# A gated linear-attention layer and its feed-forward layer: joined first products for the first two pairs of stages, the v*s term in whole blocks, and stage 0's scores ahead of the next turning

## The chip, the cores and the metric

The kernel runs on one core of one Trainium2 chip. A core has five engines that run side by side and meet through semaphores: TensorE (PE: matmuls, with weight loads listed apart as PEld), VectorE (DVE), ScalarE (ACT), GpSimd (POOL) and SyncE (SP, which here only issues transfers). The metric is the device time of one execution in microseconds, lower is better. Of several executions the median counts.

## The reference

Four sequences with eight heads of 48 channels and 768 time steps go through a recurrent attention with per-channel decay `w` and a bonus `u` for the current step; the result, brought to 3072 tokens of 384 channels, goes through two matrix products with a leaky rectifier between them.

```python
def _attn_ref(r, k, v, w, u):
    B, H, S, D = r.shape            # 4, 8, 768, 48
    state = np.zeros((B, H, D, D), dtype=np.float32)
    y = np.zeros_like(r)
    for t in range(S):
        kt, vt, rt = (k[:, :, t].copy(), v[:, :, t].copy(), r[:, :, t].copy())
        cur = np.einsum('bhd,bhe->bhde', u[None] * kt, vt)
        y[:, :, t] = np.einsum('bhd,bhde->bhe', rt, state + cur)
        state = w[None, :, :, None] * state + np.einsum('bhd,bhe->bhde', kt, vt)
    return y.astype(np.float32)

def _moe_ref(x, w_in, w_out):       # x 3072x384, w_in 384x2048, w_out 2048x384
    h = x @ w_in
    g = np.maximum(0.01 * h, h)
    return (g @ w_out).astype(np.float32)
```

## The kernel before, in words

The 3072 tokens are cut into 24 stages of 128 tokens (`NST`), six to a sequence. Two stages make a pair, and the feed-forward layer works on pairs or single stages. Within a sequence the stages hang together by a 48x48 state for each head.

A stage n goes through these steps. Their letters stand in the order that is written out by hand in `ORDER`, which covers stages 0 to 9 (the first pairs); the later pairs run in a loop of the same steps.

- `P` (`prep`, DVE): r and k times tables of powers of w. Result `qk`.
- `T` (`turn`, PE and ACT): for stages 0 to 7, eight matmuls of 128x128 against the identity (line 379) turn `qk`, four for the k half and four for the q half; two copies bring the halves from PSUM to `tp`. All copies are ACT's (line 390), except the k half of stage 0, which is DVE's (line 387). From stage 8 on a DMA transpose does the turning.
- `A` (`a_mm`, PE): the scores, eight matmuls with 48 rows each (line 403), two at a time in the upper and lower half of the array.
- `X` (`diag`, DVE): the elementwise product q*k of the turned halves; `K` (`kv_mm`, PE) sums it over channels with the bonus (four matmuls of two columns, line 433), adds k^T v (four of 96 columns, line 437) and the carried state (line 442).
- `M` (`a_mask`, DVE): the scores from PSUM times a triangular mask (line 421), two instructions of 128x512.
- `Q` (`prep2`, DVE): `vs`, that is v times the per-token, per-head sum s from `K`. `S` (`state`, DVE): the next state.
- `Y` (`y_part`, with `y_mm`, PE and ACT): the attention output of the stage, already transposed, in one PSUM bank. Its matmuls have 32 output rows each, so the array is used as four columns of 32, and four of them run side by side: 16 with the scores, 12 with the state (none where a sequence begins), and for stages 0 to 7 another 12 that add `vs` against the identity. ACT then copies the bank to `xT` (line 537).
- `G n.g` (`g1`): a quarter of the first feed-forward product for one stage, 12 matmuls of 128 columns into one bank, and one ACT instruction (the rectifier, line 555). `J m.j` (`g1_pair`): an eighth of it for both stages of pair m, six matmuls of 256 columns (line 567) and one ACT instruction (line 573). Both fill a bank of 128x512, so a `J` replaces a `G` in bank, ACT work and multiplications. `G n.g` covers what `J m.2g` and `J m.2g+1` cover, for one of the two stages. `J` needs both halves of `xT`, and needs a quarter of `w_in` as `G` does.
- `H` (`g2`): the second product of a stage, 16 matmuls of 384 columns (line 584). From pair 5 on a form with seven half-size products (line 648) does it.
- `L` loads r, k and v of a later stage; the loads of the first eight stages and of the weights are issued by POOL in the order `LOADS`, before anything else. `C`, `W` and `U` make small tables.

Each engine runs its instructions in the order in which they are recorded, so a step that waits holds up all that stands behind it on its engine. A PSUM bank is taken in turn out of eight and must have been read before it is written again. Each matmul instruction carries a weight load of its own.

Of the kernel before, what the change touches and what calls it, by code (L numbers as in the profile page):

```python
# [6 lines left out]
AF = mybir.ActivationFunctionType  # L7
# [14 lines left out]
NSL = HD // 128  # L22
# [1 line left out]
FIRST, EARLY = 6, 2  # L24
LOADS = """r1 k1 r2 id k2 wi0 v1 r3 tri k3 v2 wi1 k4 r4 v3 wi2 k5 r5 r6 k6 v4 v5 k7 wi3 r7 v6 v7 wo3 wo2 wo1 wo0"""
ORDER = """
P0 C W T0 P1 T1 A0 X0 M0 P2 A1 K0 T2 Q0 X1 Y0 A2 S0 M1 K1 X2 G0.0 Q1 P3 S1 Y1 T3 K2 M2 G1.0 X3 A3 U G0.1 S2 G1.1 Q2 M3 Y2 K3 P4
T4 Q3 G2.0 G2.1 G0.2 S3 G2.2 G1.2 Y3 P5 A4 P6 X4 M4 T5 X5 G3.0 K4 Q4 A5 S4 T6 G3.1 K5 G3.2 Y4 M5 L8 Q5 Y5 P7 A6 G1.3 J2.0 J2.1 T7
M6 X6 X7 K6 J2.2 J2.3 A7 S6 J2.4 J2.5 L9 Q6 G2.3 G0.3 J2.6 M7 L10 J2.7 L11 G3.3 K7 S7 P8 Q7 Q8 P9 H0 Q9 K8 H1 P10 L12 K9 H2 S8 S9
Y6 Y7 A8 A9 P11 M8 H3 M9 L13  # L30
"""

# [5 lines left out]
class Sched:  # L38
# [7 lines left out]

    def add(self, eng, emit, R=(), W=(), dma=None):
        o = Op()
        o.eng, o.emit, o.dma, o.inc, o.val = eng, emit, dma, False, None
        deps = []  # L50
        for key in R:
            w = self.writer.get(key)
            if w is not None:
                deps.append((w, True))
        for key in W:
            w = self.writer.get(key)
            if w is not None:
                deps.append((w, False))
            for r in self.readers.get(key, ()):
                deps.append((r, False))  # L60
        o.deps = []
        for d, raw in deps:
            if d.dma is None and d.eng == eng and dma is None and (eng == "pe" or not raw):
                continue
            if d is not o and d not in o.deps:
                o.deps.append(d)
        for key in R:
            self.readers.setdefault(key, []).append(o)
        for key in W:
            self.writer[key] = o  # L70
            self.readers[key] = []
        self.ops.append(o)
        return o
# [47 lines left out]
def bass_rwkv5_eagle__then__act_leaky_relu_kernel(  # L121
# [13 lines left out]
    def SB(name, shape, dt=BF16):  # L135
        return ctx.enter_context(nc.sbuf_tensor(name, shape, dt))

    NQK, NTP, NVS, NAT, NT, NX, NG, NO, NRK = 6, 6, 6, 6, 6, 3, 3, 4, 14
    TURNED, DIAG = 8, 8
# [29 lines left out]
    ident = SB("ident", [128, 128])  # L169
# [4 lines left out]
    tp = [SB(f"tp{i}", [128, 2 * NP, 128]) for i in range(NTP)]  # L174
    vs = [SB(f"vs{i}", [128, HD]) for i in range(NVS)]
# [12 lines left out]
    V, A, PE, SP, G = nc.vector, nc.scalar, nc.tensor, nc.sync, nc.gpsimd  # L188
    sch = Sched(ctx, nc)
    add = sch.add  # L190
    taken = [0]

    def next_bank():
        i = taken[0] % 8
        taken[0] += 1
        return ps[i], ("ps", i)
# [12 lines left out]
    def load_one(n, which, pace=()):  # L209
# [7 lines left out]
        key = (which, n if which == "v" else n % NRK)  # L217
        add("pool", lambda: G.dma_start(dst, src), R=pace, W=[key], dma=f"{which}{n}")  # L218

# [30 lines left out]
    def fill(n):  # L250
# [6 lines left out]

        add("pe", emit, R=["ones"], W=[("ps", i), f"fill{n}"])

    half_w = [(next_bank(), slice(NH * i, NH * i + NH)) for i in range(2)]  # L260

    def identity():
        add("pool", lambda: G.affine_select(ident[:, :], ones[:, 0:128], pattern=[[1, 128]], compare_op=ALU.is_equal,
                                            fill=0.0, base=0, channel_multiplier=-1), R=["ones"], W=["ident"])

# [4 lines left out]
    for name in LOADS.split():  # L270
# [12 lines left out]
        R=["tcol"], W=["kexp"])  # L283
    add("dve", lambda: V.tensor_scalar(qexp[:, :], tcol[:, :], 1.0, float(-MID), ALU.mult, ALU.add),
        R=["tcol"], W=["qexp"])
    add("dve", lambda: V.memset(v_sb[:, :, :].rearrange("p n (h e) -> p (n h) e", e=E)[:, :, D:E], 0.0), W=["v0"])
    add("dve", lambda: V.tensor_tensor(wu_row[:, :], w_row[:, :], u_row[:, :], ALU.mult),
        R=["w_row", "u_row"], W=["wu_row"])
# [5 lines left out]
    for (ps_w, key_w), cols in half_w:  # L294
        add("pe", lambda ps_w=ps_w, cols=cols: PE.matmul(ps_w[:, 0:NH], one_row[:, :], w_row[:, cols], start=True, stop=True),  # L295
            R=["one_row", "w_row"], W=[key_w, "bc"])
    for i, ((ps_w, key_w), cols) in enumerate(half_w):
        add("act", lambda ps_w=ps_w, cols=cols: A.activation(lnw[:, cols], ps_w[:, 0:NH], AF.Ln), R=[key_w], W=[("lnw", i)])
        add("act", lambda cols=cols: A.activation(qtab[:, cols], lnw[:, cols], AF.Exp, scale=qexp[:, 0:1]),
            R=[("lnw", i), "qexp"], W=[("qtab", i)])  # L300
    add("act", lambda: A.activation(ktab[:, :], lnw[:, :], AF.Exp, scale=kexp[:, 0:1]),
        R=[("lnw", 0), ("lnw", 1), "kexp"], W=["ktab"])
# [68 lines left out]
    def turn(n):  # L371
        it, iq = n % NTP, n % NQK
        for half in ((0, 1) if n == 0 else (1, 0)):
            ps_t, key = next_bank()

            def emit(half=half, ps_t=ps_t):
                for p in range(NP):
                    h0 = half * H + 2 * p
                    last = PE.matmul(ps_t[:, 128 * p:128 * p + 128],  # L379
                                     qk[iq][:, h0:h0 + 2, :].rearrange("p h e -> p (h e)"), ident[:, :],  # L380
                                     start=True, stop=True)
                return last

            add("pe", emit, R=[("kp" if half else "qp", iq), ("qk0", iq), "ident"], W=[key])
            dst = tp[it][:, NP * half:NP * half + NP, :].rearrange("p m t -> p (m t)")
            if n == 0 and half == 1:
                add("dve", lambda dst=dst, ps_t=ps_t: V.tensor_copy(dst, ps_t[:, :]),  # L387
                    R=[key], W=[("tp", it, half)])
            else:
                add("act", lambda dst=dst, ps_t=ps_t: A.activation(dst, ps_t[:, :], AF.Copy),  # L390
                    R=[key], W=[("tp", it, half)])

    def a_mm(n):
        it = n % NTP
# [100 lines left out]
    def y_mm(n, ps_y, key):  # L495
        it, ia, iv, is_ = n % NTP, n % NAT, n % NVS, n % NT

        def column(q):
            todo = []
            for s in range(NSL):  # L500
                p, kk = divmod(4 * s + q, 3)
                c0 = 128 * p
                one = []
                if kk < 2:
                    one.append((v_sb[:, n, c0 + 32 * kk:c0 + 32 * kk + 32], at[ia][:, 0, p, :]))
                if kk > 0:
                    c1 = c0 + 16 + 32 * kk
                    one.append((v_sb[:, n, c1:c1 + 32], at[ia][:, 1, p, :]))
                if n % NC:
                    one.append((st[is_][:, p, 32 * kk:32 * kk + 32], tp[it][:, p, :]))  # L510
                if n < DIAG:
                    one.append((vs[iv][:, 128 * s + 32 * q:128 * s + 32 * q + 32], ident[:, :]))
                todo += [(s, a, m, i == 0, i == len(one) - 1) for i, (a, m) in enumerate(one)]
            return todo

        def emit():
            columns = [column(q) for q in range(4)]
            for step in range(max(len(x) for x in columns)):
                for q in range(4):
                    if step < len(columns[q]):  # L520
                        s, a, m, first_mm, last_mm = columns[q][step]
                        last = PE.matmul(ps_y[32 * q:32 * q + 32, 128 * s:128 * s + 128], a, m,  # L522
                                         start=first_mm, stop=last_mm)
            return last

        reads = [("v", n), "v0", ("at", ia, 0), ("at", ia, 1), "ident", ("tp", it, 0)]
        if n < DIAG:
            reads.append(("vs", iv))
        if n % NC:
            reads.append(("st", is_))  # L530
        add("pe", emit, R=reads, W=[key])

    def y_part(n):
# [203 lines left out]
    def u_table():  # L737
# [3 lines left out]
        add("act", lambda: A.activation(u_tab[:, :], ps_u[:, 0:HD], AF.Copy), R=[key], W=["u_tab"])  # L741

    steps = {"U": u_table, "P": prep, "Q": prep2, "T": turn, "A": a_mm, "M": a_mask, "K": kv_mm, "S": state, "Y": y_part, "X": diag, "C": decay_columns, "W": decay_table, "F": fill,
             "G": g1, "J": g1_pair, "H": g2, "L": lambda n: load_stage(n, pace=[("pace", (n - 4) // 2, (n - 4) % 2)])}
    for name in ORDER.split():
# [116 lines left out]
```

## Time and profile before

| what | value |
|---|---|
| median of the runs | 169.61 us (168.82 to 169.82, 3 runs) |
| profiled execution, its own time | 169.31 us |
| profiled execution, first to last instruction (span) | 167.6 us |
| PE | 159.8 us busy, 95% of the span, 2348 matmuls and 2348 weight loads |
| DVE, ACT, POOL | 120.7, 116.1 and 81.7 us busy |
| PE's share of the chain that ended last | 93% |
| data loaded and stored by DMA | 19.68 MB |

Busy time of PE is counted from the start of a matmul to its modelled end, and one matmul starts long before the one ahead of it ends. What PE really costs is therefore read from the distance between starts: in a row such as `18.12 0.83 PE L550 ... x12` the twelve starts are spread over 0.83 us less the length of the last one. Times within the execution are microseconds from the first instruction.

### The profile page before, as it was taken

To read this page: it belongs to the slowest core of one execution; us is meant where nothing else is said; L and a number is where in the kernel's file an instruction comes from. 1 tells how busy PE (TensorE), PEld (TensorE's weight loads), DVE (VectorE), ACT (ScalarE), POOL (GpSimd) and SP (SyncE) were. 2 spreads that over 40 slices of the span, in tenths; PEclk is the share of its full clock that TensorE was granted. 3 is DMA by queue.
4 is the path that set the end of the run, shared out by engine and by line. 5 is a ranking of instruction groups with operands and counts; after the bars stand their busy time and mean duration, and the time that the engine had idled before them with its cause. 6 is when DMAs were issued, how large, how long until landed. Compare 5 with 4: busy or idle time off the path is not lost.

```text
span 167.6 us, 5494 instructions
## 1 busy us (share of the span) xinstructions
PE 159.8 (95%) x2348; PEld 133.7 (80%) x2348; DVE 120.7 (72%) x232; ACT 116.1 (69%) x264; POOL 81.7 (49%) x97
## 2 busy tenths in 40 slices
PE   6679999979999999999999999999999999999994
PEld 3557898968766885886875889889899898898993
DVE  7768884853698969999449997986998477036253
ACT  4823888778323581689989889989999845828520
POOL 7999999990079979697570660840000000000000
DMA  5999999999999999989997996994507302002022
GB/s 100 112 149 172 171 152 173 202 187 143 116 123 208 109 139 75 151 150 102 203 157 42 219 124 49 215 120 77 147 0 98 125 4 94 4 0 94 4 94 94
DMA packets 99259, 19.68 MB, mean 117 GB/s; under 512 B 92322, under 2 KB 99236, under 8 KB 99236
## 3 DMA queue, kind: packets, MB, share of 16 engines
q0 software_dynamic: 76512, 10.03, 91.6%
q1 hardware_dynamic: 21682, 9.11, 26.4%
q8 instruction: 18, 0.29, 0.7%
q10 hardware_dynamic: 1042, 0.20, 0.6%
q14 instruction: 5, 0.04, 0.1%
HBM read 20.45 MB, written 4.72 MB: 150 GB/s over the span
## 4 chain that ended last, share of the span: by engine, by line
PE 93%; DVE 3%; issue 1%; ACT 1%; DVEq 0%; ACTq 0%
PE ps_all L567 31%; PE ps_all L648 20%; PE ps_all L584 16%; PE ps_all L522 7%; PE ps_all L550 7%; PE ps_all L403 4%; PE ps_all L379 3%; PE ps_all L437 3%; DVE qk L327 1%; DVE at L421 1%; PE ps_all L255 1%; PE ps_all L442 1%; PE ps_all L295 1%; PE ps_all L433 0%; DVE tp L387 0%
## 5 line engine op out<-in xcount | busy, mean ns | idle before, releaser
L567 PE MATMUL ps_all<-xT,w_in_sb 128*128 128x256 bf16 x480 | 54.5, 273 | 0.0
L567 PEld LDWEIGHTS ps_all<-xT,w_in_sb 128*128 128x128 bf16 x480 | 46.7, 98 | 5.8
L573 ACT ACTIVATE gT<-ps_all 128x512 bf16<-128x512 f32 x80 | 46.7, 595 | 5.7 <-PE ps_all L567 2.1
L218 POOL DMA_DIRECT2D rk_sb<-in_k_dram x23 | 21.7, 944 | 16.3 <-PE ps_all L567 16.3
L584 PE MATMUL ps_all<-w_out_sb,gT 128*128 128x384 bf16 x160 | 27.2, 326 | 0.0
L413 DVE CAST_PREDICATED at<-mask,ps_all 128x1024 bf16<-128x1024 uint16 x16 | 18.8, 1219 | 8.9 <-PE ps_all L403 8.9
L367 ACT ACTIVATE at<-ident,s_tok 128x128 bf16<-128x128 bf16 x80 | 24.8, 389 | 0.0
L584 PEld LDWEIGHTS ps_all<-w_out_sb,gT 128*128 128x128 bf16 x160 | 15.3, 98 | 9.7
L218 POOL DMA_DIRECT2D v_sb<-in_v_dram x24 | 22.7, 955 | 0.4 <-issue 0.4
L218 POOL DMA_DIRECT2D rk_sb<-in_r_dram x23 | 21.5, 939 | 0.0
L361 POOL TENSOR_TENSOR at<-ident,s_tok 128x512 bf16<-128x512 bf16 x12 | 13.4, 1142 | 11.6 <-DVE s_tok L351 11.6
L679 DVE TENSOR_TENSOR out_sb<-ps_all,snap 128x192 f32<-128x192 f32 x22 | 7.8, 356 | 14.5 <-PE ps_all L648 13.8
L648 PE MATMUL ps_all<-tw,gs 128*128 128x192 bf16 x168 | 16.0, 246 | 0.0
L590 ACT ACTIVATE out_sb<-ps_all 128x384 f32<-128x384 f32 x10 | 4.9, 487 | 14.6 <-PE ps_all L584 14.6
L648 PEld LDWEIGHTS ps_all<-tw,gs 128*128 128x128 bf16 x168 | 14.0, 98 | 0.0
L421 DVE TENSOR_TENSOR at<-ps_all,mask 128x512 bf16<-128x512 f32 x16 | 10.3, 684 | 4.7 <-PE ps_all L403 4.7
L537 ACT ACTIVATE xT<-ps_all 128x384 bf16<-128x384 f32 x24 | 11.0, 490 | 3.8 <-PE ps_all L522 3.4
L550 PE MATMUL ps_all<-xT,w_in_sb 128*128 128x128 bf16 x192 | 12.9, 225 | 0.0
L550 PEld LDWEIGHTS ps_all<-xT,w_in_sb 128*128 128x128 bf16 x192 | 11.8, 101 | 0.6 <-issue 0.3
L555 ACT ACTIVATE gT<-ps_all 128x512 bf16<-128x512 f32 x16 | 9.6, 599 | 3.8 <-PE ps_all L550 3.2
L522 PE MATMUL ps_all<-at,v_sb 128*32 128x128 bf16 x384 | 11.9, 224 | 0.0
L622 DVE TENSOR_TENSOR gs<-gT 128x1024 bf16<-128x1024 bf16 x14 | 9.6, 684 | 2.9 <-ACT gT L573 2.9
(81 smaller groups left out, 241.1 us busy)
## 6 DMA issues: line engine op xcount, KB each, us to landing
out_dram<-out_sb SPq DMA_DIRECT2D x22, 192.0 KB, 2.4
v_sb<-in_v_dram POOLq DMA_DIRECT2D x24, 96.0 KB, 5.8
rk_sb<-in_r_dram POOLq DMA_DIRECT2D x23, 96.0 KB, 5.7
rk_sb<-in_k_dram POOLq DMA_DIRECT2D x23, 96.0 KB, 5.3
w_in_sb<-in_moe_w_in_dram POOLq DMA_DIRECT2D x4, 384.0 KB, 6.7
w_out_sb<-in_moe_w_out_dram POOLq DMA_DIRECT2D x4, 384.0 KB, 9.9
out_dram<-out_sb SPq DMA_DIRECT2D x4, 96.0 KB, 1.6
tp<-qk SPq DMA_TRANSPOSE x16, 3.4
```

The costliest lines, as they stand in the source:

```text
L218: add("pool", lambda: G.dma_start(dst, src), R=pace, W=[key], dma=f"{which}{n}")
L361: add("pool", lambda hh=hh, s_of=s_of: G.tensor_tensor(at[ia][:, hh, :, :], ident[:, :].unsqueeze(1).to_broadcast([128, NP, 128]), s_of.un ...
L367: add("act", lambda h=h: A.activation(at[ia][:, h % 2, h // 2, :], ident[:, :], AF.Copy, scale=s_tok[n % 2][:, h:h + 1]), R=["ident", ("s" ...
L413: add("dve", lambda: V.copy_predicated(at[n % NAT][:, :, :, :].rearrange("p two m i -> p (two m) i"), mask[:, :].bitcast(mybir.dt.uint16). ...
L421: add("dve", lambda hh=hh, part=part: V.tensor_tensor(at[n % NAT][:, hh, :, :], part, mask[:, :].unsqueeze(1).to_broadcast([128, NP, 128]) ...
L522: last = PE.matmul(ps_y[32 * q:32 * q + 32, 128 * s:128 * s + 128], a, m, start=first_mm, stop=last_mm)
L537: add("act", lambda: A.activation(xT[m % NX][:, :, 128 * half:128 * half + 128], ps_y[:, 0:HD].rearrange("p (s t) -> p s t", t=128), AF.Copy),
L550: last = PE.matmul(ps_g[:, 128 * f:128 * f + 128], w_in_sb[:, s, 128 * fb:128 * fb + 128], xT[ix][:, s, t], start=s == 0, stop=s == NSL - 1)
L567: last = PE.matmul(ps_g[:, 256 * f:256 * f + 256], w_in_sb[:, s, 128 * fb:128 * fb + 128], xT[ix][:, s, :], start=s == 0, stop=s == NSL - 1)
L573: add("act", lambda: A.activation(gT[ig][:, 2 * j:2 * j + 2, :].rearrange("p f t -> p (f t)"), ps_g[:, :], AF.Prelu, alpha=0.01), R=[key], ...
L584: last = PE.matmul(ps_o[:, 0:HD], gT[ig][:, s, 128 * half:128 * half + 128], w_out_sb[:, s, :], start=s == 0, stop=s == NFB - 1)
L648: done = PE.matmul(ps_o[:, 0:NH], lhs[:, s, :], rhs[:, s, :], start=first and s == 0, stop=s == HF - 1, skip_group_check=not (first and last))
```

## The change

Three things change, all in the first third of the execution.

1. In `ORDER`, pairs 0 and 1 get joined first products: `G0.1` to `G0.3`, `G1.1` to `G1.3` and all of `G2` and `G3` go, and `J0.2` to `J0.7` and `J1.0` to `J1.7` come. `G0.0` and `G1.0` stay. Fourteen pieces replace fourteen pieces, but they stand elsewhere: one fewer ahead of `Y2`, four fewer between `T4` and `Y3`, three more between `Y3` and `A4`, one more behind `A4`, and `J1.5` now stands between `Y5` and `A6`.
2. In `y_mm`, stages 0 to 7 no longer add `vs` in twelve matmuls of 32 output rows among the others; three matmuls with all 128 output rows follow at the end, into the same bank.
3. At the start, `P1` stands ahead of `T0`, and `A0 X0 M0` ahead of `T1`; `K0` moves ahead of `A1`. The k half of stage 0 is copied by ACT, as all others.

```diff
-P0 C W T0 P1 T1 A0 X0 M0 P2 A1 K0 T2 Q0 X1 Y0 A2 S0 M1 K1 X2 G0.0 Q1 P3 S1 Y1 T3 K2 M2 G1.0 X3 A3 U G0.1 S2 G1.1 Q2 M3 Y2 K3 P4
-T4 Q3 G2.0 G2.1 G0.2 S3 G2.2 G1.2 Y3 P5 A4 P6 X4 M4 T5 X5 G3.0 K4 Q4 A5 S4 T6 G3.1 K5 G3.2 Y4 M5 L8 Q5 Y5 P7 A6 G1.3 J2.0 J2.1 T7
-M6 X6 X7 K6 J2.2 J2.3 A7 S6 J2.4 J2.5 L9 Q6 G2.3 G0.3 J2.6 M7 L10 J2.7 L11 G3.3 K7 S7 P8 Q7 Q8 P9 H0 Q9 K8 H1 P10 L12 K9 H2 S8 S9
+P0 C W P1 T0 A0 X0 M0 T1 P2 K0 A1 T2 Q0 X1 Y0 A2 S0 M1 K1 X2 G0.0 Q1 P3 S1 Y1 T3 K2 M2 G1.0 X3 A3 U J0.2 S2 Q2 M3 Y2 K3 P4 T4 Q3
+J0.3 S3 Y3 J0.4 J0.5 J1.0 P5 A4 J1.1 P6 X4 M4 T5 X5 J1.2 K4 Q4 A5 S4 T6 J1.3 K5 J1.4 Y4 M5 L8 Q5 Y5 P7 J1.5 A6 J0.6 J2.0 J2.1 T7
+M6 X6 X7 K6 J2.2 J2.3 A7 S6 J2.4 J2.5 L9 Q6 J0.7 J1.6 J2.6 M7 L10 J2.7 L11 J1.7 K7 S7 P8 Q7 Q8 P9 H0 Q9 K8 H1 P10 L12 K9 H2 S8 S9
 Y6 Y7 A8 A9 P11 M8 H3 M9 L13
...
             dst = tp[it][:, NP * half:NP * half + NP, :].rearrange("p m t -> p (m t)")
-            if n == 0 and half == 1:
-                add("dve", lambda dst=dst, ps_t=ps_t: V.tensor_copy(dst, ps_t[:, :]),
-                    R=[key], W=[("tp", it, half)])
-            else:
-                add("act", lambda dst=dst, ps_t=ps_t: A.activation(dst, ps_t[:, :], AF.Copy),
-                    R=[key], W=[("tp", it, half)])
+            add("act", lambda dst=dst, ps_t=ps_t: A.activation(dst, ps_t[:, :], AF.Copy),
+                R=[key], W=[("tp", it, half)])
...
                 if n % NC:
                     one.append((st[is_][:, p, 32 * kk:32 * kk + 32], tp[it][:, p, :]))
-                if n < DIAG:
-                    one.append((vs[iv][:, 128 * s + 32 * q:128 * s + 32 * q + 32], ident[:, :]))
...
                         last = PE.matmul(ps_y[32 * q:32 * q + 32, 128 * s:128 * s + 128], a, m,
-                                         start=first_mm, stop=last_mm)
+                                         start=first_mm and (s == 0 or n >= DIAG),
+                                         stop=last_mm and n >= DIAG)
+            if n < DIAG:
+                for s in range(NSL):
+                    last = PE.matmul(ps_y[:, 128 * s:128 * s + 128], vs[iv][:, 128 * s:128 * s + 128], ident[:, :],
+                                     start=False, stop=s == NSL - 1)
             return last
```

## The prediction

> **What bounds the kernel now.** I read the page first: busy time, the slices, the chain that ended last.
>
> ```profile
> PE 159.8 (95%) x2348; PEld 133.7 (80%) x2348; DVE 120.7 (72%) x232; ACT 116.1 (69%) x264; POOL 81.7 (49%) x97
> PE   6679999979999999999999999999999999999994
> PE 93%; DVE 3%; issue 1%; ACT 1%; DVEq 0%; ACTq 0%
> q8 instruction: 18, 0.29, 0.7%
> ```
>
> PE sets the end from about 13 us on; the one slice below 9 between there and the end is the ninth (33.5 to 37.7 us). So a microsecond taken from PE there ends the kernel a microsecond earlier, unless a wait takes its place. What PE waits for, and the stretches around that slice:
>
> ```profile
> PE ps_all L379 <- DVE qk L329: 2.0, 2, 1.3
> PE ps_all L437 <- issue: 0.9, 1, 0.9
> 35.19 0.24 PE L437 MATMUL ps_all<-v_sb,qk 128*128 128x96 bf16 x2
> 36.35 0.24 PE L437 MATMUL ps_all<-v_sb,qk 128*128 128x96 bf16 x2 [0.93 <-issue]
> 20.00:30.00 10.00, 10.00 (x240) 9.14 (x238) 7.18 (x18) 8.42 (x17) 10.00 (x14) 1.00 2.21 163
> 30.00:35.00 5.00, 5.00 (x141) 4.47 (x139) 3.74 (x8) 3.95 (x9) 5.00 (x7) 1.00 1.31 205
> 35.00:45.00 10.00, 9.07 (x113) 7.53 (x111) 4.20 (x9) 6.78 (x12) 2.90 (x4) 1.00 2.38 147
> ```
>
> Two of the four equal matmuls of one K step run, then PE stands from the third to 36.35: starts 42 ns apart (four in 0.33 us elsewhere) would put it at 35.27, so 1.09 us are lost. No semaphore lies between them. The page has 18 instruction packets for 4696 PE instructions, some 260 each, and the stall falls just behind the densest stretch: 280 PE instructions in the 5 us to 35, against 478 in the 10 us before. I read it as PE running out of fetched instructions.
>
> Then the start, in order of time by engine:
>
> ```profile
> 7.19 0.60 ACT L390 ACTIVATE tp<-ps_all 128x512 bf16<-128x512 f32 x1
> 7.27 0.69 DVE L387 CAST tp<-ps_all 128x512 bf16<-128x512 f32 x1 [0.46 <-PE ps_all L379]
> 9.19 1.08 ACT L390 ACTIVATE tp<-ps_all 128x512 bf16<-128x512 f32 x2 [1.41 <-PE ps_all L379]
> 8.55 1.03 PE L379 MATMUL ps_all<-ident,qk 128*128 128x128 bf16 x8 [1.32 <-DVE qk L329]
> 9.52 0.61 PE L403 MATMUL ps_all<-tp 48*128 48x128 bf16 x8
> 8.73 0.34 POOL L267 TENSOR_SCALAR_AFFINE_SELECT mask<-ones 128x128 bf16<-128x128 bf16 x1
> 10.24 1.29 DVE L421 TENSOR_TENSOR at<-ps_all,mask 128x512 bf16<-128x512 f32 x2 [1.41 <-PE ps_all L403]
> 12.12 1.03 PE L379 MATMUL ps_all<-ident,qk 128*128 128x128 bf16 x8 [0.63 <-DVE qk L329]
> 15.21 1.42 PE L550 MATMUL ps_all<-xT,w_in_sb 128*128 128x128 bf16 x12
> 18.12 0.83 PE L550 MATMUL ps_all<-xT,w_in_sb 128*128 128x128 bf16 x12
> ```
>
> Stage 0's scores have both halves of `tp` at 7.96 but stand behind T1 until 9.52; the mask step, P2 and T2 (12.12) follow from them. The last two rows are the same twelve matmuls: starts 107 ns apart in the first, 56 ns in the second. Until about 16.4 us PE runs at half speed, although the granted clock reads 1.00 throughout.
>
> **The change part by part.**
>
> *The start: -0.4 us.* The k copy now follows the q copy on ACT: 7.19 + 1.08 (the two-copy row) = 8.27, against 7.96 on DVE. A0 starts at 8.3, not 9.52, and is done at 8.9; T1 follows at 8.85, 0.3 later than now, covered since P1 no longer stands behind a copy. What is late next is the mask tile, ready at 8.73 + 0.34 = 9.07, so M0 starts at 9.1 against 10.24. P2 behind it ends near 10.95; PE meanwhile waits for stage 1's copies (0.35 later than now, 10.65) and does A1, so T2 starts at 11.2 against 12.12. The lead of 0.9 us is at half speed: if PE reaches full speed at the same moment, 0.45 remain, less 0.05 because the third turning's copies stand behind two others on ACT. Bounds: 0 and -0.9.
>
> *Joined products: -0.2 us.*
>
> ```profile
> 33.32 1.47 PE L567 MATMUL ps_all<-xT,w_in_sb 128*128 128x256 bf16 x12
> ```
>
> Starts of 256 columns are (1.47 - 0.27)/11 = 109 ns apart, two of 128 columns 2 x 56 = 112. Of 192 matmuls 168 go and 84 come: 84 x 2.6 ns. ACT has as many equal instructions as before. `J0.4` needs the third block of `w_in`, issued at 14.10 and on average 6.7 us under way; it starts after 23, so that is no wait.
>
> ```profile
> 14.10 0.80 POOL L228 DMA_DIRECT2D w_in_sb<-in_moe_w_in_dram  x1
> w_in_sb<-in_moe_w_in_dram POOLq DMA_DIRECT2D x4, 384.0 KB, 6.7
> ```
>
> *Whole blocks and changed neighbours: +0.75 us.* Twelve matmuls, four abreast, are three steps of 56 ns; three whole ones take the same. What counts is the passage between shapes of the array:
>
> ```profile
> 22.57 3.51 PE L550 MATMUL ps_all<-xT,w_in_sb 128*128 128x128 bf16 x60
> 26.02 0.24 PE L522 MATMUL ps_all<-at,v_sb 128*32 128x128 bf16 x4
> 26.53 0.23 PE L522 MATMUL ps_all<-ident,vs 128*32 128x128 bf16 x4
> 26.69 0.40 PE L403 MATMUL ps_all<-tp 48*128 48x128 bf16 x8
> 27.02 0.62 PE L379 MATMUL ps_all<-ident,qk 128*128 128x128 bf16 x8
> 31.51 0.23 PE L522 MATMUL ps_all<-ident,vs 128*32 128x128 bf16 x4
> 31.64 0.24 PE L522 MATMUL ps_all<-at,v_sb 128*32 128x128 bf16 x4
> 13.70 0.32 PE L522 MATMUL ps_all<-ident,vs 128*32 128x128 bf16 x4
> 13.95 0.29 PE L403 MATMUL ps_all<-tp 48*128 48x128 bf16 x2
> ```
>
> The last of the sixty starts at 22.57 + 3.51 - 0.22 = 25.86, the first of four columns at 26.02: 0.16 instead of 0.056. Columns to half rows (26.53 to 26.69) and half rows to whole (26.87 to 27.02) are alike: 0.095 us more than a step each. Slow, it is 0.25 - 0.107 = 0.14. Where a Y stood between whole matmuls the change only moves a passage inside the step. But Y0-A2, Y3-A4, Y5-A6 and Y7-A8 were neighbours and get one passage more each, Y4-Y5 and Y6-Y7 two each: eight, one of them slow. 7 x 0.095 + 0.14 = 0.81, less 0.065, since Y4-Y5 already has 0.13 instead of 0.056, a wait for `vs` that the passage hides. A0's and T1's own passages lie in the waits at the start. No row shows a passage inside one PSUM bank's sum. Bounds: 0 if it is free there; +2.4 if each of the 24 new weight loads (101 ns, below) lies open. I stay near the rows of like passages, because 128x128 loads hide at 56 ns spacing:
>
> ```profile
> L550 PEld LDWEIGHTS ps_all<-xT,w_in_sb 128*128 128x128 bf16 x192 | 11.8, 101 | 0.6 <-issue 0.3
> ```
>
> [...]
>
> *Thinner cover: +0.9 us.* With one product fewer ahead of Y2 and four fewer behind T4, PE reaches T4 about 1 us earlier than now, but T4 needs P4, which DVE does behind stage 3's mask:
>
> ```profile
> 18.86 0.43 DVE L334 TENSOR_TENSOR prod<-tp 128x512 bf16<-128x512 bf16 x1 [0.64 <-ACT tp L390]
> 21.59 0.35 DVE L329 TENSOR_TENSOR qk<-rk_sb,tab 128x384 bf16<-128x384 bf16 x1
> 22.13 0.61 PE L379 MATMUL ps_all<-ident,qk 128*128 128x128 bf16 x8
> 27.45 1.08 ACT L390 ACTIVATE tp<-ps_all 128x512 bf16<-128x512 f32 x2 [0.15 <-PE ps_all L379]
> 28.68 0.40 PE L403 MATMUL ps_all<-tp 48*128 48x128 bf16 x8
> ```
>
> P4 ends at 21.94. DVE works without a gap from 18.86, where it waited for stage 3's copies, so it can only be as much earlier as those are: 0.3. PE then stands from about 21.2 to 21.7: 0.5. A5 waits for stage 5's copies, which end at 28.53 now and no earlier after, since J1.1's rectifier stands ahead of them on ACT; PE gets there with its lead of 0.35 and loses it. Y2 loses 0.07 to Q2. The engines that set these steps gain nothing from the moved products. Bounds: 0.25 (half of T4's wait alone) to 1.6 (if DVE is not earlier at all, 0.3, and A6 waits as A5 does, 0.4).
>
> *Instruction supply: -1.1 us.* By line, each of the eight Ys has 9 matmuls and 9 weight loads fewer, and each joined piece 6 and 6 fewer. In 30 to 35 us there lie Y4, Y5 and two or three products, so 280 becomes about 205, fewer than the 240 per 5 us that ran without a stall between 20 and 30. The stall should go. Bounds: -1.1 and 0.
>
> Sum at an unmoved change of clock: -0.4 - 0.2 + 0.75 + 0.9 - 1.1 = -0.05 us. PE is busy in one stretch from about 11.2 instead of 12.1, so full speed should come earlier too, by up to 0.9 us x 1/2; I take -0.35. Against the profiled execution's own 169.31 that gives 168.9. That execution lies 0.3 below the median of 169.61, by which it would be 169.2; I say 169.1 and count it as no change: 1% (1.7 us) is about what a measurement of this kernel can tell from none.
>
> **The rivals.**
>
> [...]
> - *The instructions still run out* (slower). Place: a K step near T7. Price 1.09. It decides if 275 PE instructions are used up faster than one packet comes in. 168.9 + 1.1 = 170.0, and 170.4 if full speed is not earlier either. Against: the counts above.
> - *Open weight loads* in the whole blocks: 24 x 0.101 = 2.4, so 168.9 + 2.4 = 171.3. Against: the 56 ns rows.
> - *The change does not cost what it says:* passages inside a bank's sum are free. 168.9 - 0.75 = 168.2. Against: the like passages.
>
> **How the numbers follow.** Forecast 0.45, early full speed 0.18, instructions run out 0.17, open weight loads 0.12, free passages 0.08. Below 167.9 lies most of the second and a little of the first and last: 0.20. Above 171.3 lies most of the fourth, and the third where thin cover reaches its 1.6: 0.20. The range 167.3 to 171.0 takes in the bounds but for the open loads.
>
> **What would show it right or wrong.** After: T2's turning near 11.2; the twelve 128-column starts of G0.0 slow still and those of G1.0 fast; 0.15 us from the last column matmul to the first whole block and 56 ns between the blocks; waits of T4 on DVE (0.5) and of A5 on ACT (0.3); no "issue" row of 0.9 on PE; row L567 x564. The stall's return, whole blocks more than 60 ns apart, or T4 without a wait would prove a term wrong.

## The result, and the profile after

The changed kernel takes 168.93 us (median of 20 runs, 168.25 to 169.48) against 169.41 us before (20 runs, 168.82 to 170.43). The ratio is 0.9966, with a 95% interval of 0.9953 to 0.9979: 0.3% faster, 0.5 us. The forecast was 169.1 us and no change beyond 1%.

The profiled execution of after took 169.43 us with a span of 167.7 us, more than the one of before (169.31 and 167.6), although the median is lower. Why is part of the reading below. The page of after, busy time, slices, chain and instruction packets:

```profile
PE 160.9 (96%) x2192; PEld 132.5 (79%) x2192; DVE 120.0 (72%) x231; ACT 116.7 (70%) x265; POOL 81.8 (49%) x97
PE   6699999999999999999999999999999999999993
PE 90%; ACT 5%; DVE 2%; issue 0%; ACTq 0%
q8 instruction: 17, 0.28, 0.7%
```

The gap in the ninth slice is gone, 156 matmuls and 156 weight loads fewer are issued, and the chain now runs through ACT for 5% of the span; the copies ahead of A0, A1, A3 and A5 make about half of that. Who held PE up, and the stretches around the old gap (PE busy and its instructions first):

```profile
PE ps_all L399 <- ACT tp L386: 1.7, 3, 1.1
PE ps_all L379 <- DVE qk L329: 0.4, 1, 0.4
20.00:30.00 10.00, 9.38 (x164) 7.48 (x162) 7.09 (x18) 7.55 (x15) 10.00 (x14) 1.00 2.20 163
30.00:35.00 5.00, 5.00 (x103) 3.90 (x102) 3.49 (x8) 3.82 (x8) 5.00 (x7) 1.00 1.33 204
35.00:45.00 10.00, 10.00 (x107) 8.21 (x105) 4.59 (x11) 7.41 (x14) 2.95 (x4) 1.00 2.37 148
```

From 20 to 30 us PE now idles 0.62 us, where it was busy throughout; from 35 to 45 us it is busy throughout, where it had idled 0.93. Instructions from 30 to 35 us fell from 280 to 205. The start, by engine:

```profile
7.21 1.08 ACT L386 ACTIVATE tp<-ps_all 128x512 bf16<-128x512 f32 x2
8.35 0.61 PE L399 MATMUL ps_all<-tp 48*128 48x128 bf16 x8 [1.11 <-ACT tp L386]
9.11 1.29 DVE L417 TENSOR_TENSOR at<-ps_all,mask 128x512 bf16<-128x512 f32 x2 [0.36 <-POOL mask L267]
11.21 1.04 PE L379 MATMUL ps_all<-ident,qk 128*128 128x128 bf16 x8
14.42 1.49 PE L549 MATMUL ps_all<-xT,w_in_sb 128*128 128x128 bf16 x12
17.87 0.83 PE L549 MATMUL ps_all<-xT,w_in_sb 128*128 128x128 bf16 x12
```

A0 starts at 8.35, the mask step at 9.11 as soon as POOL has the mask tile, T2 at 11.21. The first twelve products are slow, the second twelve fast, as before. In this execution the last slow matmul starts at 16.79; before it was at 16.28. Slow means at the spacing of 107 ns for 128 columns; behind it the spacing is 56 ns, and that change is called full speed below. One joined product, the passages within Y4 and from Y4 to Y5, and the two new waits:

```profile
19.40 0.83 PE L566 MATMUL ps_all<-xT,w_in_sb 128*128 128x256 bf16 x6
31.34 0.23 PE L516 MATMUL ps_all<-tp,st 128*32 128x128 bf16 x4
31.50 0.34 PE L521 MATMUL ps_all<-ident,vs 128*128 128x128 bf16 x3
31.77 0.24 PE L516 MATMUL ps_all<-at,v_sb 128*32 128x128 bf16 x4
21.11 0.33 PE L438 MATMUL ps_all<-st,ident 128*128 128x384 bf16 x1
21.83 0.62 PE L379 MATMUL ps_all<-ident,qk 128*128 128x128 bf16 x8 [0.40 <-DVE qk L329]
28.15 0.33 PE L438 MATMUL ps_all<-st,ident 128*128 128x384 bf16 x1
28.70 0.40 PE L399 MATMUL ps_all<-tp 48*128 48x128 bf16 x8 [0.22 <-ACT tp L386]
```

From the last column matmul to the first whole block lie 0.16 us, the three blocks start 0.06 apart ((0.34 - 0.22)/2), and it takes another 0.16 us to the next stage's columns. T4 starts 0.72 us after the K step's last matmul, which takes PE 0.16, so it waits 0.56; A5 starts 0.55 after its predecessor instead of 0.26 (0.16 and the passage of 0.095), so it waits 0.29.

### The profile page after: what moved, and what is told of

Its sections match the earlier page's. It is cut to its first block, busy times and chain, and to the rows that moved or that the text cites. A ratio compares the mean times of both kernels' runs of the same rounds, so it can differ in the third digit from the quotient of the medians.

```text
span 167.7 us, 5182 instructions
## 1 busy us (share of the span) xinstructions
PE 160.9 (96%) x2192; PEld 132.5 (79%) x2192; DVE 120.0 (72%) x231; ACT 116.7 (70%) x265; POOL 81.8 (49%) x97
## 3 DMA queue, kind: packets, MB, share of 16 engines
q1 hardware_dynamic: 21682, 9.11, 25.3%
## 4 chain that ended last, share of the span: by engine, by line
PE 90%; ACT 5%; DVE 2%; issue 0%; ACTq 0%
PE ps_all L566 36%; PE ps_all L647 20%; PE ps_all L583 16%; PE ps_all L516 6%; PE ps_all L399 5%; ACT tp L386 2%; PE ps_all L433 2%; PE ps_all L379 2%; PE ps_all L521 1%; PE ps_all L549 1%; DVE at L417 1%; PE ps_all L255 1%; PE ps_all L295 1%; ACT tab L299 1%; ACT wl L474 0%
## 5 line engine op out<-in xcount | busy, mean ns | idle before, releaser
L566 PE MATMUL ps_all<-xT,w_in_sb 128*128 128x256 bf16 x564 | 64.8, 273 | 0.0
L566 PEld LDWEIGHTS ps_all<-xT,w_in_sb 128*128 128x128 bf16 x564 | 54.5, 98 | 6.9 <-issue 0.2
L572 ACT ACTIVATE gT<-ps_all 128x512 bf16<-128x512 f32 x94 | 55.1, 597 | 6.6 <-PE ps_all L566 2.8
L647 PE MATMUL ps_all<-w_out_sb,gT 128*128 128x192 bf16 x112 | 11.6, 246 | 0.0
L516 PE MATMUL ps_all<-at,v_sb 128*32 128x128 bf16 x384 | 11.4, 228 | 0.0
L386 ACT ACTIVATE tp<-ps_all 128x512 bf16<-128x512 f32 x16 | 8.7, 596 | 3.7 <-PE ps_all L379 3.6
L399 PE MATMUL ps_all<-tp 48*128 48x128 bf16 x192 | 8.8, 228 | 1.8 <-ACT tp L386 1.7
```

The costliest lines, as they stand in the source:

```text
L399: last = PE.matmul(at_bank[n][hh][0][:, 128 * p:128 * p + 128], tp[it][rows, NP + p, :], tp[it][rows, p, :], start=True, stop=True)
L566: last = PE.matmul(ps_g[:, 256 * f:256 * f + 256], w_in_sb[:, s, 128 * fb:128 * fb + 128], xT[ix][:, s, :], start=s == 0, stop=s == NSL - 1)
L572: add("act", lambda: A.activation(gT[ig][:, 2 * j:2 * j + 2, :].rearrange("p f t -> p (f t)"), ps_g[:, :], AF.Prelu, alpha=0.01), R=[key], ...
L647: done = PE.matmul(ps_o[:, 0:NH], lhs[:, s, :], rhs[:, s, :], start=first and s == 0, stop=s == HF - 1, skip_group_check=not (first and last))
```

## The experiments

All times are medians; ratios are against before, run alongside on the same chip.

### One part at a time

`start_only` is before with the new start, `blocks_only` before with the whole blocks, `joined_only` before with after's order from `U` on, `no_blocks` is after with the old `y_mm`. Dots stand for code that is not shown.

```diff
 start_only
-P0 C W T0 P1 T1 A0 X0 M0 P2 A1 K0 T2 ...
+P0 C W P1 T0 A0 X0 M0 T1 P2 K0 A1 T2 ...      (and stage 0's k copy on ACT)
 blocks_only
-                if n < DIAG:
-                    one.append((vs[iv][:, 128 * s + 32 * q:128 * s + 32 * q + 32], ident[:, :]))
...
+            if n < DIAG:
+                for s in range(NSL):
+                    last = PE.matmul(ps_y[:, 128 * s:128 * s + 128], vs[iv][:, 128 * s:128 * s + 128], ident[:, :], ...
 joined_only
-X3 A3 U G0.1 S2 G1.1 Q2 M3 Y2 K3 P4 T4 Q3 G2.0 G2.1 G0.2 S3 G2.2 G1.2 Y3 P5 A4 ...
+X3 A3 U J0.2 S2 Q2 M3 Y2 K3 P4 T4 Q3 J0.3 S3 Y3 J0.4 J0.5 J1.0 P5 A4 J1.1 ...
 no_blocks (against after)
+                if n < DIAG:
+                    one.append((vs[iv][:, 128 * s + 32 * q:128 * s + 32 * q + 32], ident[:, :]))
...
-            if n < DIAG:
-                for s in range(NSL):
-                    last = PE.matmul(ps_y[:, 128 * s:128 * s + 128], vs[iv][:, 128 * s:128 * s + 128], ident[:, :], ...
```

> Before, with the new start alone (P1 ahead of T0, A0 X0 M0 ahead of T1, K0 ahead of A1, stage 0's k copy on ACT). By the sum: T2 near 11.2 us, -0.4 to -0.5 us against before, and the 1 us row of issue near T7 stays, since PE has as many instructions as before (about 275 of them used up in 5 us at that place). Rival, the stall hangs on the moment and not on the count of instructions: it goes, -1.5 us. Rival, the start's lead is lost in later waits: 0.

> Before, with the whole blocks of v*s alone. By the sum: one passage more at Y0-A2, Y3-A4, Y5-A6, Y7-A8 and two at Y4-Y5 and Y6-Y7, +0.7 us; 0.15 us from the last column matmul to the first whole block, 56 ns between the blocks. 108 PE instructions fewer by 35 us, so the stall near T7 goes (-1.1), though a shorter one may come one packet earlier, near Y4: -0.4 to +0.7 in all. Rival, weight loads lie open: +2.4. Rival, a passage inside one bank's sum is free: -1.1.

> Before, with the joined products and their places alone. By the sum: -0.2 from the starts of 109 instead of 112 ns, about +1.0 from T4 waiting for DVE, A5 and A3 for ACT, -1.1 because the stall near T7 goes (275 instructions in 6.8 us or more everywhere): 0 +- 0.3 us. Rival, cover is not thinner: -1.3. Rival, the stall stays: +1.0.

> After, with v*s in columns of 32 as before, so start and joined products without the whole blocks. By the sum: the eight passages go, -0.5 us against after (about -1.0 against before), with no stall (275 instructions in 6.8 us or more). Rival, whole blocks are free or a gain: equal to after or slower.

| kernel | median us | ratio, 95% interval | profiled span us | last slow matmul starts us |
|---|---|---|---|---|
| start_only | 168.87 | 0.9958, 0.9937 to 0.9979 | 166.7 | 15.47 |
| blocks_only | 169.23 | 0.9993, 0.9976 to 1.0009 | 167.0 | 15.54 |
| joined_only | 169.73 | 1.0000, 0.9981 to 1.0018 | 167.3 | 16.07 |
| no_blocks | 168.26 | 0.9933, 0.9909 to 0.9957 | 166.0 | 14.30 |

In `start_only` the stall stands in the same place, before the third of K6's four matmuls:

```profile
34.33 0.24 PE L433 MATMUL ps_all<-v_sb,qk 128*128 128x96 bf16 x2
35.44 0.24 PE L433 MATMUL ps_all<-v_sb,qk 128*128 128x96 bf16 x2 [0.87 <-issue]
```

It came 0.91 us earlier and had not gone; in these two executions it follows the count of instructions, not the moment. In the three kernels with fewer PE instructions the list of PE's waits has no such row. What the parts do is best seen in the starts of some steps on PE, each in one profiled execution:

```
        before  joined_only   after  no_blocks  start_only  blocks_only   cover  before_fill
T2       12.12        12.12   11.21      11.21       11.20        12.12   11.21        12.12
T4       22.13        21.92   21.83      20.60       21.26        21.91   21.30        20.94
A5       28.68        28.78   28.70      27.46       27.82        28.57   27.22        27.49
K6       35.08        35.93   35.96      34.61       34.22        35.22   34.25        36.05
A7       37.84        37.60   37.64      36.28       36.93        36.89   35.93        37.72
H0       43.24        42.96   43.00      41.64       42.33        42.30   41.29        43.12
A8       52.54        52.26   52.62      50.94       51.63        51.92   50.59        52.42
span    167.57       167.31  167.69     165.99      166.68       166.98  165.67       167.48
```

The rows must be read with the moment of full speed, which scatters from execution to execution. Where PE sets the pace, a shift of it is worth half its length, since starts are 107 ns apart before it and 56 after. `start_only` leads by 0.91 at H0; full speed came 0.8 earlier, worth 0.4, so the start itself gives 0.5. `joined_only` loses 0.85 up to K6 and wins 1.09 with the stall. `blocks_only` leads by 0.94: stall -1.09, full speed -0.37, passages about +0.5. `no_blocks` lies 1.68 ahead of after at A8, of which full speed (2.5 us earlier) makes 1.25; about 0.4 are the whole blocks. These are single executions. The -0.6 us that the trace of `blocks_only` leaves without full speed is more than its median shows: 0.1 us below before, with an interval from 0.4 below to 0.2 above.

### Is it the supply of instructions?

In `quiet_dma` the transfer queues are nearly empty in the stretch ahead of the stall's place: from 30 to 34 us the DMA engines move at most 25 GB/s in any one us, the instruction packet in it included, against 201 to 218 in before. The part of the data that is left out is named in the expectation.

```diff
 quiet_dma (against before)
-        add("pool", lambda: G.dma_start(w_out_sb[:, 4 * i:4 * i + 4, :], wout_view[:, 4 * i:4 * i + 4, :]),
+        add("pool", lambda: G.memset(w_out_sb[:, 4 * i:4 * i + 4, :], 0.0), W=[("wout", i)])
...
+        if 8 <= n < 12:
+            add("pool", lambda: G.memset(dst, 0.0), R=pace, W=[key])
+            return
```

> Before, but w_out and stages 8 to 11's r, k and v are filled with zeros by POOL instead of loaded, so that no load is under way from about 31 to 50 us; part of the data is left out, every PE instruction stays. If PE stands near T7 because its next packet of instructions comes late through busy transfer queues, the packet asked for at 30 us arrives before 34 and the 0.9 us row of issue goes: one profiled time near 168.2. If the stall has another cause (something in PE's own order), it stays.

One time, 167.79 us (span 166.0; last slow matmul at 15.22). K6's four matmuls follow each other, with every PE instruction where it was before (the lines are two further down):

```profile
34.60 0.24 PE L435 MATMUL ps_all<-wu,prod 128*128 128x2 bf16 x4
34.70 0.33 PE L439 MATMUL ps_all<-v_sb,qk 128*128 128x96 bf16 x4
34.87 1.36 PE L569 MATMUL ps_all<-xT,w_in_sb 128*128 128x256 bf16 x11
```

The trace's fourth instruction packet (16 KB) came from 33.95 to 34.84 in before, and from 31.26 to 32.21 here. PE came to the instruction 256 ahead of the stall's place, by the counts further down, at 30.79 in before and at 30.31 here: 0.5 us earlier, and the packet came 2.7 us earlier. So the stall is a packet that comes late while loads fill the queues; one execution without the loads shows it, and the counts below bear it out.

### Filling the two waits, and the gaps of the start

```diff
 cover (against no_blocks)
-... Y2 K3 P4 T4 Q3 J0.3 S3 Y3 J0.4 J0.5 J1.0 P5 A4 J1.1 P6 X4 M4 T5 X5 J1.2 K4
+... Y2 K3 P4 J0.3 T4 Q3 S3 Y3 J0.4 J0.5 J1.0 P5 A4 P6 X4 M4 T5 J1.1 X5 J1.2 K4
 after_fill (against after), cover_fill (against cover)
-P0 C W P1 T0 A0 X0 M0 T1 P2 K0 A1 T2 ...
+P0 C F1 W P1 T0 F2 A0 X0 M0 T1 P2 K0 F1 A1 T2 ...
```

`F n` is the step that is there already for the first two matmuls: n matmuls of 512 columns on ones.

> Start and joined products without the whole blocks, and the two waits of the thinner cover are filled: J0.3 ahead of T4, and T5 ahead of J1.1. By the sum T4 no longer waits for P4 (0.5) nor A5 for stage 5's copies (0.3 to 0.35): -0.8 to -1.2 us against the same kernel with after's order, about 167.3 in the median. Rival: the wait only moves to the next step (Y3 for vs, or DVE as a whole is the bound there): no change. A stall of instructions may come back near 31 us, since 275 instructions are used up in 6.3 us: then half of the gain.

> The same with four matmuls of 512 columns on constants in PE's gaps of the start (one ahead of T0, two between T0 and A0, one ahead of A1), whose results nobody reads. If full speed is earned by a stretch without gaps, it comes before 9 us instead of 14 to 17, and the steps to about 22 us are then bound by DVE, ACT and loads: -0.6 to -1.5 us against the same kernel without them. If the moment is tied to something else, no change or +0.2.

> After, with the same four matmuls on constants and nothing else. If a stretch without gaps earns full speed: all 128-column starts 56 ns apart from before 9 us on, about -1.5 us against after (167.4). If not: no change.

`cover` takes 167.57 us (4 runs), ratio 0.9882 (0.9861 to 0.9903); 0.5% or 0.9 us below `no_blocks`, each against its own runs of before. The waits of T4 and A5 are gone from its trace, but its profiled execution is only 0.35 us ahead of that of `no_blocks` at A8, because K3 waits for stage 3's v:

```profile
PE ps_all L429 <- DMA v_sb<-in_v_dram: 0.5, 1, 0.5
```

K3 stands ahead of the pieces that `cover` moves, so this wait is not T4's in a new place: the load, issued at the same time, landed at 20.16 in this execution and at 19.16 in that of `no_blocks`.

`after_fill` takes 167.87 us, ratio 0.9900 (0.9880 to 0.9921), against 0.9966 for after. Its turnings on PE:

```profile
8.88 1.04 PE L379 MATMUL ps_all<-ident,qk 128*128 128x128 bf16 x8
11.04 0.62 PE L379 MATMUL ps_all<-ident,qk 128*128 128x128 bf16 x8
```

Eight matmuls in 0.62 us instead of 1.03: full speed is there by 10.7 us instead of 17. The gain, 0.66% or 1.1 us, is less than the 1.5 expected and than the half of 6 us; the list of PE's waits now has 1.0 us for a block of `w_in` and 0.6 for stage 3's v, so loads hold the start. `cover_fill` takes 166.92 us, ratio 0.9840 (0.9818 to 0.9862), the best of all: 1.6% below before and 0.7 us below `cover` by the two ratios.

### The same matmuls in before and in start_only

```diff
 before_fill (against before)
-P0 C W T0 P1 T1 A0 X0 M0 P2 A1 K0 T2 ...
+P0 C F1 W T0 F3 P1 T1 A0 X0 M0 P2 F1 A1 K0 F2 T2 ...
 start_fill (against start_only), no_blocks_fill (against no_blocks)
-P0 C W P1 T0 A0 X0 M0 T1 P2 K0 A1 T2 ...
+P0 C F1 W P1 T0 F2 A0 X0 M0 T1 P2 K0 F1 A1 T2 ...
```

> Before, with matmuls of 512 columns on constants in PE's gaps of the start (one ahead of T0, three ahead of T1, one ahead of A1, two ahead of T2), whose results nobody reads. Full speed by about 9 to 11 us, as in the other kernel with such matmuls; the stall near T7 stays. 7 us less of half speed, of which the waits of the start take part: -1.3 to -1.8 us against before. If the lower level of before were only chance of the moment, no change.

> Before with the new start alone and constant matmuls in its gaps: full speed by 9 to 11 us, the stall stays. With the moment of full speed out of the comparison, the start's own lead shows against before with such matmuls: -0.6 us (T2 0.9 earlier, part of it lost in a wait for loads), so about -2.2 against before.

> Start and joined products without the whole blocks, with constant matmuls in the gaps. Against the start alone with them: thinner cover +1.1, no stall -1.1, so 0 +- 0.3. Against after with such matmuls (167.87 measured elsewhere): -0.4 to -0.7, the price of the whole blocks' passages. If the joined products truly gain, lower than the start alone by 0.5 or more.

`before_fill`: 169.43 us, ratio 0.9989 (0.9972 to 1.0007). Against the expectation nothing was gained, although full speed came by 10.8 us. PE's waits and two rows of its time say where the gain went:

```profile
PE ps_all L433 <- issue: 1.3, 1, 1.3
PE ps_all L550 <- issue: 0.6, 1, 0.6
12.12 0.62 PE L379 MATMUL ps_all<-ident,qk 128*128 128x128 bf16 x8 [0.27 <-DVE qk L329]
30.00 0.62 PE L550 MATMUL ps_all<-xT,w_in_sb 128*128 128x128 bf16 x8 [0.57 <-issue]
36.05 0.24 PE L433 MATMUL ps_all<-wu,prod 128*128 128x2 bf16 x4 [1.33 <-issue]
```

Counted in matmuls, weight loads and the semaphore instructions between them, 961 PE instructions stand ahead of the first stall and 1217 ahead of the second; that is 256 apart, near the 261 for each of the page's 18 packets (4696 over 18), so about one packet of 16 KB (0.29 MB over 18). The one stall of before and of `start_only` is also behind 1217, and the two of `start_fill` are behind 961 and 1217. All six stalls end 1.4 to 1.5 us after a packet has landed. In `before_fill` PE came 0.79 us earlier to the instruction 256 ahead of the later stall (30.00, against 30.79 in before), but the fourth packet came only 0.3 us earlier (33.62 to 34.56, against 33.95 to 34.84). In the table above it is 1.2 us ahead at T4 and A5 and 0.1 at A7. Not every lead is lost so: in `start_only` the fourth packet came at 33.05 and the lead of 0.9 us went through the stall whole; in `start_fill`, with PE 0.5 us further ahead at the instruction 256 ahead of the stall, it came at 33.03. POOL issues the same loads at the same times to 0.1 us in all four kernels, so its pace alone does not say why the new start moved the packets and the matmuls on constants hardly did; that stays open.

`start_fill`: 168.50 us, ratio 0.9938 (0.9914 to 0.9962), with stalls of 1.4 and 0.6 us; the lead over `before_fill` is 0.9 us (0.6 expected), the gain over before half of what was expected. `no_blocks_fill`: 167.21 us, ratio 0.9875 (0.9841 to 0.9909), with no stall: 0.6% or 1.1 us below `start_fill` by the two ratios, where the same time was expected, and 0.4 us below `after_fill`, as expected. By the ratios the matmuls on constants gained 0.66% in after, 0.58% in `no_blocks` and 0.42% in `cover`, which have fewer PE instructions, and 0.20% in `start_only` and 0.11% in before, which have not. In this stretch an earlier PE paid most where no packet was late.

## Why the prediction was right, by its own steps

- **The start, -0.4 us.** A0 at 8.35 (8.3 forecast), the mask as the next late thing (9.11; 9.1), T2 at 11.21 (11.2). Measured with the moment of full speed taken out: -0.5.
- **Joined products.** Six starts of 256 columns in (0.83 - 0.27)/5 = 0.11 us each; the -0.2 is an amount worked out, too small to be measured by itself. The 564 matmuls of 256 columns are as forecast, one line further up (L566).
- **Passages, +0.75 us.** 0.16 us at each, and no weight load lies open (0.06 between whole blocks), so that rival falls, and so does the one with free passages. But the step put all eight to the whole blocks. Y3-A4 and Y5-A6 are also parted by the new order, as `joined_only` has it without any whole block. The blocks alone cost 0.4 to 0.7 us: 0.4 by the traces of `no_blocks` and after, 0.6 by their ratios (168.26 against 168.93 us by the medians), 0.4 by the ratios with full speed early in both (167.21 against 167.87), where the two intervals overlap.
- **Thinner cover, +0.9 us.** T4 waits 0.56 (0.5 forecast), A5 0.29 (0.35), Y2 not at all (0.07). Filling them gave 0.9 us in `cover` by the medians; its one trace shows 0.35, with the late load that is named above.
- **Instruction supply, -1.1 us.** The stall went, 205 instructions from 30 to 35 us as worked out, and `quiet_dma` shows the cause in one execution (packet 2.7 us earlier, no stall). The slower rival did not come about.
- **The sum at an unmoved clock, -0.05 us.** The two profiled spans differ by +0.11; after's full speed came 0.5 us later, worth +0.25 at half: -0.14. The sum holds where it can be read, in one execution of each.
- **Full speed earlier, -0.35 us.** This step is the weakest. The one profile of after shows it later, not earlier. The last slow matmul started at 16.79, 15.47, 14.30 and 14.30 in the four kernels with the new start (after, `start_only`, `no_blocks`, `cover`), at 16.28, 15.54, 16.07 and 15.22 in the four with the old one (before, `blocks_only`, `joined_only`, `quiet_dma`): 0.6 earlier on the mean, with a scatter larger than that. The median's -0.5 us against a sum of -0.05 agrees with it; it is not shown. So the sum's -0.4 may have come near the measured -0.5 by luck, since most of it is this term. That full speed follows the beginning of PE's unbroken work, from which the term was taken, is the author's estimate, and no run shows it for the new start; what the runs showed is that the matmuls on constants brought the change to between 9 and 12 us in all five kernels that had them. Early full speed, which the chances give 0.18, did not come about in after (16.79); the earliest of the other three with its start was 14.30, 2.0 us ahead of before.

What the prediction did not see is that the terms do not add freely: in before, the time that the matmuls on constants won ahead of 30 us is lost again at the late packets. The step "a microsecond taken from PE there ends the kernel a microsecond earlier, unless a wait takes its place" had this wait in its last words, and `before_fill` is that case. What `joined_only` does by itself is settled only to its interval of 0.3 us either way.

## What to carry to other kernels

An idle stretch on PE with no releaser, in the middle of a step (1.09 us lost in before), is worth a count of instructions against the instruction packets (256 between two stalls here); fewer and longer matmuls were worth more there than their array time (in `joined_only` the 1.09 us went, against the 0.2 worked out for the starts), and a kernel whose PE came earlier to such a stall won nothing in one case (`before_fill`, 1.2 us ahead at A5 and 0.1 at A7) and kept its lead in another (`start_only`, 0.9). Matmuls of the same shape belong next to each other: each change of shape cost 0.1 us at full speed here (starts 0.16 us apart instead of 0.06), so by estimate a filler moved between two like steps costs that as well as its cover. Compare profiles only after reading where full speed set in, for one execution's moment was worth more (1.25 us between after and `no_blocks`) than the whole change.

## What the runs showed of the hardware that was not expected

- An instruction packet of 16 KB landed 4.1 us (before, 30.79 to 34.84) to 4.6 us (`before_fill`, 30.00 to 34.56) after PE came to the instruction 256 ahead of the one it then stood at, while loads filled the queues, and 1.9 us after it when they did not (`quiet_dma`, 30.31 to 32.21). That the packet is asked for at this instruction is read from the counts, not shown.
- Four or seven matmuls on constants in PE's idle time moved full speed from between 14 and 17 us to between 9 and 12 us and won 1.1 us in after and nothing beyond the interval in before (0.9989, 0.9972 to 1.0007).
- The moment of full speed differs by 2.5 us (14.30 to 16.79) between single executions of four kernels that start alike, which at half its shift is about 1.2 us in the result. The runs of before spread over 1.6 us (168.82 to 170.43); whether this moment makes that spread is not shown.
